# Spreading the third batch's norm and w_in's maxima over the partitions by way of DRAM instead of TensorE

## The chip, the cores and the metric

The kernel runs on one core of a Trainium2 chip. The metric is the time of one execution on the device in microseconds, median of several runs. PE stands for TensorE, DVE for VectorE, ACT for ScalarE, POOL for GpSimd and SP for the engine whose queue issues most of the DMAs.

## The reference, cut to what matters

```
# q, k, v: 8 batches x 8 heads x 576 x 64;  p: 8 x 8 x 32 x 64
def sm_attn(qq, kk, vv):                     # softmax(qq kk^T / 8) vv
    ...
p_packed = sm_attn(p, k, v)                  # 32 packed rows a head
x = sm_attn(q, p_packed, p_packed)           # 576 rows a head
h = x @ w_in                                 # 4608 x 512 @ 512 x 2048
g = h * erf(softplus(h))
out = g @ w_out                              # 4608 x 2048 @ 2048 x 512
```

All of it is float32 (the weights arrive as 64 bit floats and are cut down on the chip).

## The kernel before, in words

The second attention is a product of small softmax weights (`a2`, 128 x 576 twice) with the packed rows, so the kernel multiplies the packed rows into `w_in` first (`w_prime`, line 599: tiles `wp`) and then forms h as `a2` times `wp` (`h_half`, line 650). Each float32 operand is split into a high and a low part (`wph` and `wpl`, `a2h` and `a2l`, `gh` and `gl`, `woh`), and three products are summed. Batches 0 and 1 use a float32 format for the parts; from batch 2 on (`NB0 = 2`, "the third batch") the parts are float16, which needs scales: powers of two that come from the largest absolute norm of the packed rows and the largest entry of `w_in`.

The feed-forward part is a list of units. A unit is one batch, one half of its 576 rows and 256 of the 2048 hidden columns. `step(n, m)` (line 750) issues two groups of six matmuls for h of unit n, copies them from PSUM by ACT, issues the 24 output matmuls (`o_part`, line 711) of unit m = n - 5, and the split of g for unit m + 2. ACT's softplus and erf, and DVE's product (line 692), stand between. Units 20 to 23 are the second row half of batch 0 with hidden blocks 4 to 7 (so `gh_1_6` in the lists below belongs to unit 22), units 24 to 27 the first row half of batch 1 with the same blocks.

What else has to happen (the attention of later batches, the scales, loads of weights) is put into slots of units by a table, `slot(n, where)`. From unit 20 on nothing but the order of these calls, and a scheduler that works by a simulated time, sets the order in each engine's queue; the order in a queue is kept on the chip. Tiles come from pools: h and some scores share the two banks of `ps_h`, `wp` and the second half of the scores use `ps_m`, `gh` and `gl` have two buffers each.

The scale needs a maximum over the 128 partitions, known in every partition. `spread` (line 188) does this without PE: DVE transposes the column in blocks of 32, SP writes the four rows of 32 to DRAM (line 193, `line`), and SP reads them back into a row that is the same in all partitions (line 195, `row`). Then `two_over` (line 175) takes the row's maximum and makes a power of two of it, three DVE instructions (lines 177, 178, 180). Batches 3 to 7 and `w_out`'s maxima (`col_out`, `line_out`, `row_out`) go this way. The third batch's norm and `w_in`'s maxima (`top_in`) are turned on PE by two transposes (lines 547 and 204) into the bank `po`, from which DVE takes the maximum.

`scales(b)` (line 212) makes `rho`, `back` and `gs` from the two inverses. `w_prime_high` (line 631) multiplies by `rho` on ACT for batch 2 (line 636, `wph`), and `w_prime_low` does the same on DVE (line 645, `wpl`).

SP's queue holds, around this work, the loads of `q` for batch 2, then eight loads of 512 KB of `w_out` back from DRAM (`wox<-scratch`, line 238), then `p`, `k` and `v` of batch 3. The transfers of this queue count on eight semaphores in turn, so a transfer is issued when the one eight places ahead of it has landed.

Of the kernel before, what the change touches and what calls it, by code (L numbers as in the profile page):

```python
# [8 lines left out]
F32 = mybir.dt.float32  # L9
# [36 lines left out]
def tile_pack_attention_moe(ctx: ExitStack, tc: tile.TileContext, qT, kT, v, pT, w_in, w_out, outT):  # L46
    nc = tc.nc
    P = 128
# [17 lines left out]
    NB0 = 2  # L66
# [8 lines left out]
    cpool = ctx.enter_context(tc.tile_pool(name="const", bufs=1))  # L75
# [9 lines left out]
    ident = cpool.tile([P, P], F32, name="ident")  # L85
# [72 lines left out]
    tops, inverse, halved, pairs = {}, {}, {}, {}  # L158
# [16 lines left out]
    def two_over(dst, src):  # L175

        nc.vector.tensor_reduce(dst, src, axis=AX.X, op=ALU.max)
        nc.vector.tensor_scalar(dst, dst, TINY, None, op0=ALU.max)
        bits = dst.bitcast(U32)
        nc.vector.tensor_scalar(bits, bits, EXPONENT, EXPONENT, op0=ALU.bitwise_and, op1=ALU.bitwise_xor)  # L180

    def gather(kind):

        top = cpool.tile([P, 1], F32, name=f"top_{kind}")
        nc.vector.tensor_reduce(top[:], tops[kind][:], axis=AX.X, op=ALU.max)
        halved[kind] = top if kind == "in" else spread(kind, top[:])

    def spread(name, column):

        wide = apool.tile([P, NK], F32, name=f"col_{name}", tag="col", bufs=1)  # L190
        nc.vector.transpose(wide[:], column.to_broadcast([P, NK]))
        line = dpool.tile([P // NK, NK], F32, name=f"line_{name}", tag="line", bufs=2)
        nc.sync.dma_start(line[:], wide[:].rearrange("(q k) n -> q k n", k=NK)[:, 0, :])
        row = apool.tile([P, P], F32, name=f"row_{name}", tag="row", bufs=1)
        nc.sync.dma_start(row[:], line[:].rearrange("q n -> (q n)").unsqueeze(0).to_broadcast([P, P]))
        return row[:]

    def turn(kind, row=None):

        if row is None:  # L200
            inverse[kind] = cpool.tile([P, 1], F32, name=f"inv_{kind}")
            two_over(inverse[kind][:], halved[kind])
            return
        nc.tensor.transpose(row, halved[kind][:].to_broadcast([P, P]), ident[:])
        inverse[kind] = cpool.tile([P, 1], F32, name=f"inv_{kind}")
        two_over(inverse[kind][:], row)

    def other_way(dst, src):

# [64 lines left out]
    def is_narrow(b, j):  # L274

        return b >= NB0 + 2 or (b == NB0 + 1 and j >= 2)

    functions = []

# [66 lines left out]
    def attention(b):  # L346

        joined, third, roomy = b > NB0, b == NB0, b == 0
# [10 lines left out]
        def bank(name, single=False):  # L359

            if single:
                return [ps_h.tile([P, 512], F32, name=f"{name}_{b}_{x}", tag="ps_h")[:] for x in range(2)], None
            if name in at_o:
                d = at_o[name]
                return [ps_o.tile([P, 512], F32, name=f"{name}_{b}_{x}", tag=f"ps_o{d + x}")[:] for x in range(2)], None
            ps = ps_m.tile([P, 2, 512], F32, name=f"{name}_{b}", tag="ps_m")
            return [ps[:, 0, :], ps[:, 1, :]], ps
# [98 lines left out]
        if roomy:  # L466
# [7 lines left out]
            po, pr = bank("p")[0]  # L474
# [11 lines left out]
        else:  # L486
# [9 lines left out]
            if joined:  # L496
# [10 lines left out]
                po, pr = bank("p")[0]  # L507
# [28 lines left out]
        if b >= NB0:  # L536
# [3 lines left out]
            norm = apool.tile([P, 1], F32, name=f"norm{b}", tag="norm")  # L540
            nc.vector.tensor_reduce(norm[:], norms[:], axis=AX.X, op=ALU.max)
            if joined:
                norm_row = spread(b, norm[:])
        yield
        nc.tensor.transpose(pr[:, 2 * P:3 * P], pn, ident[:])
        if third:
            nc.tensor.transpose(po[:, P:2 * P], norm[:].to_broadcast([P, P]), ident[:])
        if b == NB0:
            turn("in", po[:, 2 * P:3 * P])
        yield  # L550
        ptt = apool.tile([P, P], F32, name=f"pt{b}", tag="pt")
        nc.scalar.copy(ptt[:], pr[:, 2 * P:3 * P])
        pt[b] = ptt
        def pack_pairs():
            inverse[b] = apool.tile([P, 1], F32, name=f"inv{b}", tag="inv")
            two_over(inverse[b][:], po[:, P:2 * P] if third else norm_row)
            if third:
                return
            sp = apool.tile([P, 1], F32, name=f"sp{b}", tag="sp")
            nc.vector.tensor_scalar(sp[:], inverse[b][:], 2.0 ** 13, None, op0=ALU.mult)  # L560
            pt16[b] = apool.tile([P, 2, P], F16, name=f"pt16_{b}", tag="pt16")
            nc.vector.tensor_scalar(pt16[b][:, 0], ptt[:], sp[:], None, op0=ALU.mult)
            nc.vector.scalar_tensor_tensor(pt16[b][:, 1], ptt[:], sp[:], pt16[b][:, 0], op0=ALU.mult, op1=ALU.subtract)

        if third:
            pack_pairs()
        yield
        ta = apool.tile([P, 2, S], F32, name=f"ta{b}", tag="big", bufs=3)
        for c2 in range(2):
            banks = bank(f"s2_{c2}", b > NB0 + 1 or (b >= NB0 and c2 == 0) or (b == 1 and c2 == 1))  # L570
            for c in range(NC):
                for r in range(2):
                    nc.tensor.matmul(banks[0][r][NK * c:NK * c + NK, 0:HT], ptt[64 * r:64 * r + 64, NK * c:NK * c + NK],  # L573
                                     q[c][64 * r:64 * r + 64, c2 * HT:(c2 + 1) * HT], start=True, stop=True)
            yield
            if roomy:
                scores.append(banks[0])
            else:
                for r in range(2):
                    nc.vector.transpose(ta[:, r, c2 * HT:(c2 + 1) * HT], banks[0][r][:, 0:HT])  # L580
                if joined and c2 == 1:
                    pack_pairs()
                yield
        tb = apool.tile([P, 2, S], F32, name=f"tb{b}", tag="big", bufs=3)
        kind = F32R if b < NB0 else F16
# [13 lines left out]
    def w_prime(b, j):  # L599

        f0, n = PIECES[j]
        if (b, j) in BESIDE:
            ps = [ps_h.tile([P, 512], F32, name=f"wp{b}_{j}_{r}", tag="ps_h") for r in range(2)]
        else:
            ps = ps_m.tile([P, 2, 512], F32, name=f"wp{b}_{j}", tag="ps_m")
            ps = [ps[:, r, :] for r in range(2)] + [ps]
        terms = ((0, 0), (0, 1), (1, 0)) if is_narrow(b, j) else (None,)
        for m, term in enumerate(terms):
            for c in range(NC):
                for r in range(2):  # L610
                    rows = slice(64 * r, 64 * r + 64)
                    if term:
                        fo = f0 % (2 * FB)
                        p, w = pt16[b][rows, term[0]], narrow[c, f0 // (2 * FB)][rows, term[1], fo:fo + n]
                    else:
                        p, w = pt[b][rows], w_in_sb[rows, c, f0:f0 + n]
                    nc.tensor.matmul(ps[r][NK * c:NK * c + NK, 0:n], p[:, NK * c:NK * c + NK], w,  # L617
                                     start=(m == 0), stop=(m == len(terms) - 1), skip_group_check=len(terms) > 1)
        raw[b, j] = ps
# [11 lines left out]
    def w_prime_high(b, j, copy=nc.scalar.copy):  # L631
        for hi, lo, ps in w_prime_parts(b, j):
            if b < NB0:
                copy(hi, ps)
            elif b == NB0 or (b, j) in BESIDE:
                nc.scalar.mul(hi, ps, 2.0 ** -15 if is_narrow(b, j) else rho[b][:])
            else:
                nc.vector.tensor_scalar(hi, ps, 2.0 ** -15 if is_narrow(b, j) else rho[b][:], None, op0=ALU.mult)
# [153 lines left out]
    def attend(b):  # L792
        if b not in gens:
            gens[b] = attention(b)
        next(gens[b])

    def slot(n, where):
        return plan.setdefault((n, where), [])
# [14 lines left out]
    f = 2  # L813
# [4 lines left out]
    for n, kind in ((22, "in"), (27, "out")):  # L818
        slot(n, 1).append((gather, kind))
    slot(28, 5).append((turn, "out"))  # L820
    slot(24, 2).append((scales, NB0))
    slot(28, 5).append((out_weights,))
    slot(32, 3).append((out_scale, NB0))
    for i, high, low in ((0, 28, 29), (1, 28, 30), (2, 29, 30), (3, 30, 31), (4, 31, 32), (5, 32, 33), (6, 32, 35), (7, 34, 37)):
# [106 lines left out]
```

## Time and profile before

| | us |
|---|---|
| median of 3 runs | 676.59 (676.27 to 678.91) |
| profiled execution | 677.14 |
| its span, first to last instruction | 675.4 |
| PE busy | 663.9 (98%) |
| DVE busy | 516.7 (77%) |
| ACT busy | 504.6 (75%) |
| POOL busy | 69.8 (10%) |

The busy share of DVE and ACT is a mean over the whole span. Between 160 and 170 us, where the third batch's scale is used, DVE is busy for 9.86 of 10 us and ACT for 9.58. The page's chain that ended last lies on PE for 84% of the span and on DVE for 7%.

### The profile page before, as it was taken

The numbers are of one execution on the slowest core, as the hardware profiler recorded it, in microseconds if no ns is written. First come the engines' busy times: TensorE is split into PE (matmuls) and PEld (weight loads), VectorE is DVE, ScalarE is ACT, GpSimd is POOL, SyncE is SP. The second block draws the span as 40 slices with busy tenths as digits, with TensorE's granted clock in tenths as the row PEclk, the third lists the DMA queues.
The fourth block names the chain that finished last, engine by engine and source line by source line (L and its number), as shares of the span: only waits on it lengthen the run. The fifth ranks groups of instructions, "written<-read, shape, count | busy, mean of one in ns | idle before, by whom it ended". The sixth has DMA issues, their size and how long they took to land.

```text
span 675.4 us, 15725 instructions
## 1 busy us (share of the span) xinstructions
PE 663.9 (98%) x6530; PEld 531.9 (79%) x6530; DVE 516.7 (77%) x836; ACT 504.6 (75%) x814; POOL 69.8 (10%) x103
## 2 busy tenths in 40 slices
PE   8999999999999999999999999999999999999998
PEld 5687999998988777777777777777777777777776
DVE  4999999988997689879976769567885768563443
ACT  2799988877779679667786878766796777777681
POOL 2032033102433100100010000100001000000000
PEclk9999999999999999999999999999999999999999
DMA  9996457249244703520052303322033100001011
GB/s 314 401 352 221 149 170 267 84 155 309 32 125 64 185 1 106 162 71 29 7 172 94 95 1 98 98 81 86 2 135 98 36 1 12 27 1 36 1 36 36
DMA packets 40503, 73.44 MB, mean 109 GB/s; under 512 B 4976, under 2 KB 17840, under 8 KB 40432
## 3 DMA queue, kind: packets, MB, share of 16 engines
q1 hardware_dynamic: 34832, 61.29, 27.7%
q0 software_dynamic: 5312, 10.56, 6.1%
q8 instruction: 51, 0.84, 0.5%
q10 hardware_dynamic: 288, 0.59, 0.2%
q14 instruction: 20, 0.16, 0.1%
HBM read 53.48 MB, written 18.94 MB: 107 GB/s over the span
## 4 chain that ended last, share of the span: by engine, by line
PE 84%; DVE 7%; ACT 3%; issue 3%; DMA 3%; POOL 1%; SPq 0%; POOLq 0%; ACTq 0%; DVEq 0%
PE o L722 52%; PE h L667 25%; PE wp L617 3%; DMA wi<-w_in 2%; PE p L450 1%; DVE hs L692 1%; PE s L573 1%; DMA k<-kT 1%; DVE gl L705 1%; PE s L420 1%; DVE w_in_sb L117 1%; DVE a2l L343 1%; DVE tops_in L165 1%; ACT L685 0%; DVE wpl L643 0%
## 5 line engine op out<-in xcount | busy, mean ns | idle before, releaser
L722 PE MATMUL o<-gh,woh 128*128 128x288 f16 x1536 | 301.0, 287 | 0.0
L722 PEld LDWEIGHTS <-woh 128*128 128x128 f16 x2304 | 223.8, 98 | 64.5 <-issue 8.8
L722 PE MATMUL o<-gl,woh 128*128 128x288 f16 x768 | 219.9, 286 | 0.0
L667 PE MATMUL h<-a2h,wph 128*128 128x288 f16 (+1 forms) x512 | 149.1, 291 | 1.0 <-DVE hs L677 0.6
L667 PE MATMUL h<-a2h,wpl 128*128 128x288 f16 (+1 forms) x512 | 147.9, 289 | 1.2 <-DVE wpl L643 1.2
L667 PE MATMUL h<-a2l,wph 128*128 128x288 f16 (+1 forms) x512 | 147.7, 289 | 0.0
L698 DVE CAST gh<-hs 128x576 f16<-128x576 f32 (+1 forms) x117 | 53.2, 455 | 98.8 <-PE o L722 98.5
L679 ACT ACTIVATE hs<-h 128x288 f32<-128x288 f32 x168 | 64.5, 406 | 85.1 <-PE h L667 85.1
L722 PE MATMUL o<-gh,wohl 128*128 128x288 f32 x448 | 98.7, 300 | 0.4 <-ACT ob L732 0.2
L705 DVE TENSOR_TENSOR gl<-hs,gh 128x576 f16<-128x576 f32 (+1 forms) x124 | 95.5, 770 | 4.5 <-ACT gh L698 0.5
L692 DVE TENSOR_TENSOR hs<-t,hs 128x576 f32<-128x576 f32 x128 | 91.6, 761 | 1.3 <-ACT t L688 1.2
L667 PEld LDWEIGHTS <-wph 128*128 128x128 f16 x768 | 74.3, 98 | 20.2 <-issue 1.0
L722 PEld LDWEIGHTS o<-gh,wohl 128*128 128x128 f32 x448 | 74.4, 188 | 7.2 <-issue 2.7
L688 ACT ACTIVATE t<-t 128x576 f32<-128x576 f32 x128 | 79.5, 674 | 0.6
L685 ACT ACTIVATE t<-hs,gs 128x576 f32<-128x576 f32 x96 | 74.5, 776 | 3.8 <-DVE hs L677 1.6
L685 ACT ACT_TABLE_LOAD x50 | 64.2, 1283 | 5.4 <-DVE hs L677 3.6
L722 PE MATMUL o<-gl,wohl 128*128 128x288 f32 x224 | 66.3, 296 | 0.1
L688 ACT ACT_TABLE_LOAD x49 | 62.9, 1283 | 0.9
L667 PEld LDWEIGHTS <-wpl 128*128 128x128 f16 x384 | 37.6, 98 | 9.5
L722 PEld LDWEIGHTS o<-gl,wohl 128*128 128x128 f32 x224 | 42.3, 189 | 0.3 <-DVE gl L705 0.3
L734 ACT ACTIVATE ob<-o,omega 128x288 f32<-128x288 f32 x48 | 21.8, 493 | 15.3 <-PE o L722 15.3
L501 POOL DMA_DIRECT2D a1m<-wide x20 | 11.8, 593 | 201.1 <-DMA wide<-a 150.5
(135 smaller groups left out, 750.2 us busy)
## 6 DMA issues: line engine op xcount, KB each, us to landing
q<-qT SPq DMA_DIRECT2D x32, 288.0 KB, 3.8
k<-kT SPq DMA_DIRECT2D x30, 288.0 KB, 5.3
wos<-w_out SPq DMA_DIRECT2D x16, 512.0 KB, 4.7
v<-v SPq DMA_DIRECT2D x29, 256.0 KB, 3.9
outT<-ob SPq DMA_DIRECT2D x48, 144.0 KB, 1.8
wi<-w_in SPq DMA_DIRECT2D x12, 512.0 KB, 7.1
outT<-ob POOLq DMA_DIRECT2D x32, 144.0 KB, 3.8
scratch<-wo POOLq DMA_DIRECT2D x16, 256.0 KB, 2.9
```

The lines of the kernel that those rows point to most:

```text
L117: nc.vector.scalar_tensor_tensor(bits, middle, 13, bits, op0=ALU.logical_shift_right, op1=ALU.bitwise_or)
L501: queue.dma_start(moved[NK * x:NK * x + NK, r], wide[r][:, t0:t0 + NCH * NK].rearrange("(c k) t -> k c t", k=NK))
L617: nc.tensor.matmul(ps[r][NK * c:NK * c + NK, 0:n], p[:, NK * c:NK * c + NK], w, start=(m == 0), stop=(m == len(terms) - 1), skip_group_che ...
L667: nc.tensor.matmul(ps[:, 0:HT], w[:, r, fo:fo + P], a[:, r, c * HT:(c + 1) * HT], start=(m == 0), stop=(m == 5))
L679: nc.scalar.mul(dst, src, 2.0 ** -18)
L685: in_turn(nc.scalar.activation(ts[n][:], rows[n][:], AF.Softplus, scale=scale))
L688: in_turn(nc.scalar.activation(ts[n][:], ts[n][:], AF.Erf))
L692: nc.vector.tensor_tensor(hs[:], ts.pop(n)[:], hs[:], op=ALU.mult)
L698: copy(ghi[:], gs[n][0][:])
L705: nc.vector.tensor_tensor(glo[:], hs[:], ghi[:], op=ALU.subtract)
L722: nc.tensor.matmul(acc[b, c, d][:, 0:HT], w[f][:, d * P:(d + 1) * P], gg[:, k, :], start=(first and k == 0 and m == 0), stop=(last and k = ...
L734: nc.scalar.mul(ob[:], acc[b, c, d][:, 0:HT], omega[b][:])
```

## The change

The norm of the third batch and the maxima of `w_in` now also go through `spread`. PE's two transposes disappear, `turn` loses its branch for PE, and `gather` calls `spread` for both kinds. `w_in`'s column is turned right after its maxima are gathered (unit 22). In the attention of the third batch, in the yield that held `pack_pairs()`, DVE now makes `w_in`'s inverse and then turns the norm's column. The norm's inverse and `scales` move from slot (24, 2) to slot (25, 1), ahead of the `wph` of slot (25, 2).

```
-        halved[kind] = top if kind == "in" else spread(kind, top[:])
+        halved[kind] = spread(kind, top[:])
...
-    def turn(kind, row=None):
-
-        if row is None:
-            inverse[kind] = cpool.tile([P, 1], F32, name=f"inv_{kind}")
-            two_over(inverse[kind][:], halved[kind])
-            return
-        nc.tensor.transpose(row, halved[kind][:].to_broadcast([P, P]), ident[:])
+    def turn(kind):
+
         inverse[kind] = cpool.tile([P, 1], F32, name=f"inv_{kind}")
-        two_over(inverse[kind][:], row)
+        two_over(inverse[kind][:], halved[kind])
...
+    packs = {}
+
+    def pack(b):
+
+        packs.pop(b)()
...
         nc.tensor.transpose(pr[:, 2 * P:3 * P], pn, ident[:])
-        if third:
-            nc.tensor.transpose(po[:, P:2 * P], norm[:].to_broadcast([P, P]), ident[:])
-        if b == NB0:
-            turn("in", po[:, 2 * P:3 * P])
...
-            two_over(inverse[b][:], po[:, P:2 * P] if third else norm_row)
+            two_over(inverse[b][:], norm_row)
...
         if third:
-            pack_pairs()
+            turn("in")
+            norm_row = spread(b, norm[:])
+            packs[b] = pack_pairs
...
-    slot(24, 2).append((scales, NB0))
+    slot(25, 1).append((pack, NB0))
+    slot(25, 1).append((scales, NB0))
```

Three places show what this moves. The first is SP's queue behind the last load of batch 2's `q`. Before, the loads of `w_out` follow at once:

```order
L407 DMA q_2_1646<-qT 128x576
L238 DMA wox_1880<-scratch 128x2x512
L238 DMA wox_1882<-scratch 128x2x512
L238 DMA wox_1985<-scratch 128x2x512
L238 DMA wox_1987<-scratch 128x2x512
L238 DMA wox_2078<-scratch 128x2x512
```

After the change the write of `w_in`'s column (`line_in`) stands ahead of them and the read of its row (`row_in`) behind the fourth:

```order
L408 DMA q_2_1646<-qT 128x576
L193 DMA line_in<-col_in 4x32
L233 DMA wox_1886<-scratch 128x2x512
L233 DMA wox_1888<-scratch 128x2x512
L233 DMA wox_1991<-scratch 128x2x512
L233 DMA wox_1993<-scratch 128x2x512
L195 DMA row_in<-line_in 128x128
L233 DMA wox_2084<-scratch 128x2x512
```

Two small transfers have come into the row of eight large ones.

The second place is the same queue behind the eighth `wox`. Before, it holds batch 3's first loads (and a `p` of batch 4), and then the pair for `w_out`'s maxima:

```order
L379 DMA p_2205<-pT 128x128
L382 DMA k_3_2207<-kT 128x576
L382 DMA k_3_2208<-kT 128x576
L379 DMA p_3005<-pT 128x128
L382 DMA k_3_2209<-kT 128x576
L382 DMA k_3_2210<-kT 128x576
L402 DMA v_3_2585<-v 64x512
L402 DMA v_3_2588<-v 128x512
L193 DMA line_out<-col_out 4x32
L195 DMA row_out<-line_out 128x128
```

After, the pair for the third batch's norm (`line` and `row`) stands among them, with two `k` and two `v` between its halves:

```order
L380 DMA p_2215<-pT 128x128
L383 DMA k_3_2217<-kT 128x576
L383 DMA k_3_2218<-kT 128x576
L380 DMA p_3015<-pT 128x128
L193 DMA line_2028<-col_2026 4x32
L383 DMA k_3_2219<-kT 128x576
L383 DMA k_3_2220<-kT 128x576
L403 DMA v_3_2595<-v 64x512
L403 DMA v_3_2598<-v 128x512
L195 DMA row_2030<-line_2028 128x128
L193 DMA line_out<-col_out 4x32
L195 DMA row_out<-line_out 128x128
```

The read of the row is the last but two of these twelve.

The third place is DVE's queue where the scale is worked out. Before, `rho` needs only what is already in SBUF, and the maxima of `w_out` (`tops_out`) come behind it:

```order
L319 TENSOR_REDUCE mx_2118<-ta_2052 128x36
L321 TENSOR_TENSOR ta_2052<-ta_2052,mx_2118 128x1152
L215 TENSOR_SCALAR rho_2121<-inv_2022,inv_in 128x1
L210 TENSOR_SCALAR back_2123<-rho_2121 128x1
L219 TENSOR_SCALAR gs_2125<-back_2123 128x1
L165 TENSOR_REDUCE tops_out<-wohl_1310 128x1
L165 TENSOR_REDUCE tops_out<-wohl_1331 128x1
L165 TENSOR_REDUCE tops_out<-wohl_1336 128x1
L698 CAST gh_1_6_2190<-hs_1_6_1843 128x576
```

After, the three maxima come first, then the norm's inverse from the row that comes from DRAM, then `rho`:

```order
L322 TENSOR_TENSOR ta_2058<-ta_2058,mx_2124 128x1152
L165 TENSOR_REDUCE tops_out<-wohl_1310 128x1
L165 TENSOR_REDUCE tops_out<-wohl_1331 128x1
L165 TENSOR_REDUCE tops_out<-wohl_1336 128x1
L177 TENSOR_REDUCE inv_2163<-row_2030 128x1
L178 TENSOR_SCALAR inv_2163<-inv_2163 128x1
L180 TENSOR_SCALAR inv_2163<-inv_2163 128x1
L210 TENSOR_SCALAR rho_2167<-inv_2163,inv_in 128x1
L205 TENSOR_SCALAR back_2169<-rho_2167 128x1
L214 TENSOR_SCALAR gs_2171<-back_2169 128x1
L697 CAST gh_1_6_2200<-hs_1_6_1843 128x576
```

The inverse of `w_in` has moved likewise: it stood ahead of the split of unit 20's g, and now stands behind it, with the turn of the norm's column, right ahead of the four transposes of the second scores (`ta<-s`, line 580). ACT's queue has the same instructions in the same order.

## Rows read from the trace of the kernel before

**Rows 1.** Page, busy us and share of the span, by engine

```profile
PE 663.9 (98%) x6530; PEld 531.9 (79%) x6530; DVE 516.7 (77%) x836; ACT 504.6 (75%) x814; POOL 69.8 (10%) x103
```

**Rows 2.** Chain that ended last, in order of time: start us, us, what

```profile
149.69 0.32 PE p L547
150.01 0.11 PE p L204
150.12 0.80 PE o L722 x6
```

**Rows 3.** Timeline of PE: start us, us, engine line op out<-in xcount

```profile
149.18 0.33 PE L545 MATMUL p<-ident,a 128*128 128x128 f32 x1
...
156.85 0.29 PE L667 MATMUL h<-a2h,wph 128*128 128x288 f32 x1
...
167.59 0.30 PE L667 MATMUL h<-a2h,wph 128*128 128x288 f32 x1
```

**Rows 4.** Timeline of SP's queue, DMA issues

```profile
145.24 5.10 SPq L238 DMA_DIRECT2D wox<-scratch  x8
...
155.13 0.33 SPq L379 DMA_DIRECT2D p<-pT  x1
...
161.43 0.34 SPq L402 DMA_DIRECT2D v<-v  x1
...
221.99 0.52 SPq L193 DMA_DIRECT2D line<-col  x1
227.89 0.33 SPq L195 DMA_DIRECT2D row<-line  x1
```

**Rows 5.** What SP's queue waited for, 150 to 162 us: total, times, longest

```profile
SPq L382 <- DMA wox<-scratch: 3.9, 4, 1.0
...
SPq L379 <- DMA wox<-scratch: 1.7, 2, 0.9
```

**Rows 6.** Issues at 152.47 and 155.13: KB, us from issue to landing

```profile
k<-kT SPq DMA_DIRECT2D x1, 288.0 KB, 11.3
...
p<-pT SPq DMA_DIRECT2D x1, 64.0 KB, 10.5
```

**Rows 7.** Landing of the six reads of a row, line 195

```profile
DMA to landing us min/median/max: 2.8/2.9/4.3
```

**Rows 8.** Busy time by stretch: PE, PEld, DVE, ACT, POOL, clock, DMA share, GB/s

```profile
167.00:169.00 2.00, 2.00 (x17) 2.00 (x16) 1.97 (x4) 1.99 (x3) 0.00 (x0) 1.00 0.20 61
```

**Rows 9.** Timeline of DVE

```profile
154.06 1.58 DVE L580 STREAM_TRANSPOSE ta<-s 128x288 f32<-128x288 f32 x4 [1.27 <-PE s L573]
...
161.38 1.86 DVE L165 TENSOR_REDUCE tops_out<-wohl 128x1 f32<-128x512 f32 x3
...
178.72 0.28 DVE L177 TENSOR_REDUCE inv_out<-row_out 128x1 f32<-128x128 f32 x1 [0.73 <-DMA row_out<-line_out]
...
179.42 0.15 DVE L231 TENSOR_SCALAR sigma<-inv_out 128x1 f32<-128x1 f32 x1
```

**Rows 10.** Timeline of ACT

```profile
162.81 1.09 ACT L636 ACTIVATE wph<-wp,rho 128x1024 f16<-128x1024 f32 x1
...
166.28 0.68 ACT L675 COPY hs<-h 128x288 f32<-128x288 f32 x2
```

**Rows 11.** Timeline of PE, its start and its last matmul

```profile
1.35 4.52 PE L860 MATMUL idle<-ident 128*128 128x128 f32 x22 [1.35 <-POOL ident masks.py:199]
...
17.24 2.95 PE L860 MATMUL idle<-ident 128*128 128x128 f32 x24
...
671.76 0.29 PE L722 MATMUL o<-gh,woh 128*128 128x288 f16 x1
```

**Rows 12.** Busy time by stretch at the end, columns as in rows 8

```profile
672.00:674.00 2.00, 0.04 (x1) 0.00 (x0) 0.00 (x0) 0.50 (x1) 0.00 (x0) 1.00 0.61 218
674.00:675.40 1.40, 0.00 (x0) 0.00 (x0) 0.00 (x0) 0.00 (x0) 0.00 (x0) 0.56 0.00 0
```

## The prediction, before the changed kernel ran

> **What bounds the kernel now.** I read the page's busy shares first. PE is busy for 663.9 of 675.4 us [rows 1], so a microsecond that PE loses in the middle of the program is lost at the end, and nearly nothing is there to make it good. Then I read the chain in order of time around the edit, to see whether PE's two removed transposes lie on it: they do [rows 2]. Then the timelines of PE, DVE, ACT and of SP's queue between 145 and 180 us, because the change takes little from PE and puts two round trips through DRAM in its place. The reader is to see three things there. PE starts the six plus six h matmuls of unit 25 at 156.85 and those of unit 27 at 167.59 [rows 3]. ACT makes the first `wph` with the scale at 162.81, and only behind it, in order, the copies of unit 26's h out of PSUM, at 166.28 [rows 10]. And SP's queue is in its fullest stretch: eight loads of 512 KB are issued within 5.1 us from 145.24 [rows 4], and each later issue waits for one of them to land [rows 5].
>
> **What it removes.** PE's transpose of pn ends at 149.18 + 0.33 = 149.51; behind it come the norm's transpose (which waited for DVE) and the one of the maxima, and the output matmuls go on at 150.12 [rows 2, 3]. Without both they go on at 149.51, so PE gains 0.61 us. ACT's copy of pt comes earlier too, which is worth nothing, since PE uses it 3 us later.
>
> **What it adds: the first round trip.** Two SP transfers, `line_in` (0.5 KB) and `row_in` (64 KB). Issuing takes about 0.5 and 0.33 us [rows 4], beside other work. What counts is the landing. A pair in the other loaded stretch shows it: the write of the column was issued at 221.99, and the read of the row, which only waits for that landing, at 227.89, so 512 bytes took over 5 us behind the loads ahead of them [rows 4]. The read itself took 2.8 us at best and 4.3 at worst [rows 7]. So small transfers here land in the order of the queue, after what is ahead of them. `row_in` stands behind the fourth `wox`, which landed at 155.1: the `p` issued at 155.13 had waited for it [rows 4, 5]. For 64 KB I add 0.4 us, as k's landing (152.47 + 11.3 = 163.8) and p's (155.13 + 10.5 = 165.6) have 352 KB in 1.8 us between them [rows 6]. With the pipe's end the row is there at 155.6; bounds are 150.6 (issued at 147.8 behind four issues, 2.8 us) and 156.5.
>
> DVE needs it behind gl of unit 20, at about 151.6, and stands until 155.6. Behind the wait on DVE are three small instructions (178.72 to 179.42 in the same sequence before, 0.70 us) and the column's turn (0.25 us), then the four transposes of the scores, which started at 154.06 and were idle 1.27 us before [rows 9]; they now start at 156.6. They free the two banks that unit 25's h uses: the first at 157.0. PE would be there at 156.85 - 0.61 = 156.24 [rows 3], so it waits 0.8 us, and the gain is gone by unit 25 (0.15 us behind the old kernel). At the early bound PE does not wait and keeps 0.61.
>
> **The second round trip.** It is `line`, `row`, the inverse and then `rho`. `line` needs the column's turn and the landing of the transfer eight places ahead, the fifth `wox`, so it goes out at about 157, behind the first two `k` and the `p`, which landed as late as 165.6 [rows 6]; it uses few rings, so I give it 164 to 166. `row` stands behind two more `k` and two `v` in the queue, and eight places behind the first `k`, which landed at 163.8; with the added 64 KB, 164.1. So SP issues `row` at 164.1 to 166, and it lands 2.8 to 4.3 us later [rows 7]: 166.9 to 170.3. I take 169.0, an issue at 164.7 plus 4.3, because the two `k` and two `v` are then still in the rings: before, the engines were busy for 0.20 of the stretch from 167 to 169, that is until about 167.4, with the last `v` issued at 161.43 [rows 4, 8], and the two reads add 128 KB.
>
> DVE gets to the inverse at about 165.5 (the three maxima ended at 161.38 + 1.86 = 163.2 [rows 9], 0.5 us of scale work is no longer ahead of them, and all is 2.5 us late from the transposes). It stands until 169.0. The inverse takes 0.70 and rho 0.21 with its gaps 0.26, so `wph` starts on ACT at 169.96 instead of 162.81. Queued behind it on ACT are the table load and the exp of the scores, and then the copies of unit 26's h, 166.28 - 162.81 = 3.47 us after wph's start [rows 10], the first done 0.37 later. PE's h of unit 27 needs those two banks. So it starts at 169.96 + 3.84 = 173.8, against 167.59: **6.2 us late**, the 0.61 and the 0.8 included. The bounds of the row give 171.7 (4.1 late) and 175.1 (7.5). DVE's split of unit 22 and `wpl` are late too, but done at about 171.6 and 174.9, ahead of PE's use of them. From there PE is the bound again; DVE is some 1.4 us behind it and has the slack of a unit, price nothing to 1.4.
>
> **The clock.** PE would be ready at 167.59 + 0.15 and stand for about 6 us. TensorE's last matmul ends at 672.05; the stretch from 672 to 674 still has a granted clock of 1.00, the level of 2.4 GHz, and that from 674 to 675.4 a mean of 0.56, so the lower level (1.2 GHz) came at about 674.2, 2.1 us after the last matmul [rows 11, 12]. At the start the first 22 dummy matmuls took 4.52 us and later 24 of them 2.95 [rows 11]: 123 ns at the upper level, hence 246 at the lower, and 4.52 us are 14.7 at the lower level, 3.6 us. So a stand of 6 us costs another half of 3.6, 1.8 us. The Trainium skill (TensorE: Matmul & The Clock Gate, What's actually happening) says that the lower level is the default and that activity lifts it. By the middle of this trace alone, where no stand is that long, the term would be nothing and the sum 6.2; by that rule it is due, and the two ends of the trace agree with it.
>
> **Sum.** 6.2 + 1.8 = 8.0 us on the profiled execution's 677.14 (span 675.4 and 1.7 around it): 685.1. The median of the runs is 0.55 lower, so 684.6.
>
> **The rivals.** *The small transfers are not held up by the large ones.* Then `row_in` lands at 150.6, PE keeps its 0.61 through unit 25, but `row` still cannot be issued before the first `k` landed, 164.1, and lands at 166.9. PE's unit 27 starts at 171.7, 4.1 late, with the clock's 1.8 only in part: 680.7 to 682.5. For it: the median of the six rows is 2.9 [rows 7]; against it: 221.99 to 227.89 [rows 4]. [...]
>
> *The scale is in time, and only the transposes' removal is left.* This is the case that isn't slower. Its place is ACT's copy of unit 26; it decides by the landing of `row`: at 162.2 or before, the copies end before 167.0 and PE waits for nothing. It then gains 0.61 us, 676.0. Against it: eight issues in turn on landings that the trace shows [rows 5]; for it: only if the large loads ahead run earlier than before.
>
> *The stand is longer or the clock costs double.* `line` lands behind the following k as well, `row` at 170.3, and the lower level lasts through two stretches of 3.6 us: 7.5 + 3.6, 687.7.
>
> **Numbers.** The forecast has 0.68, the first rival 0.15, the second 0.10, the third 0.07. What a measurement of this kernel can tell from no change is 0.5%, 3.4 us. The forecast, the first and the third lie above 680.0, all but a corner of the first; the second lies within. Faster by over 3.4 us has no mechanism, 0.02 for what I have not seen. Slower 0.88, within 0.10. The range goes from the first rival's early end, 680.4, to 687.8, the third's.
>
> **What would show it.** DVE idle before `inv<-row` (line 177) for over 2 us with the row's DMA named; `wph` of line 635 at 168 us or later; PE idle for 4 to 6 us before unit 27's h, released by ACT's copies, and a clock under 1.00 in the stretch behind it; about 4 us of DVE idle before `inv_in<-row_in`. The prediction is wrong if `wph` starts before 165, or if PE has no idle time over 1 us between 150 and 180.

## The result, and the profile after

The changed kernel takes a median of 685.87 us (684.52 to 686.91, four runs) against 676.43 for the kernel before (675.83 to 678.91, four runs): a ratio of 1.0136, 95% interval 1.0123 to 1.0150. It is slower by 1.4%, and the forecast of 684.6 (680.4 to 687.8) holds. The profiled execution took 685.98, with a span of 684.2, 8.8 longer than before.

Read the changed kernel first as the kernel before was read, by the page's busy line. PE is busy 3.8 us more [rows 1] with two instructions fewer:

```profile
PE 667.7 (98%) x6528; PEld 534.9 (78%) x6528; DVE 517.5 (76%) x838; ACT 504.8 (74%) x814; POOL 68.6 (10%) x103
```

The work is the same less two transposes, so the longer busy time is time in which PE worked slowly; what else the 8.8 holds is time in which it stood. The timeline of SP's queue, which answers to [rows 4], shows the four small transfers between the large ones (start, issue time, count):

```profile
145.21 0.62 SPq L193 DMA_DIRECT2D line_in<-col_in  x1
145.92 2.06 SPq L233 DMA_DIRECT2D wox<-scratch  x4
148.35 1.98 SPq L195 DMA_DIRECT2D row_in<-line_in  x1
150.42 2.20 SPq L233 DMA_DIRECT2D wox<-scratch  x4
153.51 0.35 SPq L380 DMA_DIRECT2D p<-pT  x1
...
158.69 0.51 SPq L193 DMA_DIRECT2D line<-col  x1
...
165.08 1.38 SPq L403 DMA_DIRECT2D v<-v  x2
166.56 0.38 SPq L195 DMA_DIRECT2D row<-line  x1
```

In DVE's timeline the two rows are what its two longest waits of this stretch end on:

```profile
157.37 0.28 DVE L177 TENSOR_REDUCE inv_in<-row_in 128x1 f32<-128x128 f32 x1 [5.75 <-DMA row_in<-line_in]
...
158.07 1.53 DVE L579 STREAM_TRANSPOSE ta<-s 128x288 f32<-128x288 f32 x4
...
170.54 0.29 DVE L177 TENSOR_REDUCE inv<-row 128x1 f32<-128x128 f32 x1 [4.17 <-DMA row<-line]
...
171.24 0.21 DVE L210 TENSOR_SCALAR rho<-inv,inv_in 128x1 f32<-128x1 f32 x1
```

ACT, waiting for `rho`, makes `wph` at 171.54 instead of 162.81, and the copies of unit 26's h come 3.50 us behind it, as they did before (3.47) [rows 10]:

```profile
171.54 1.11 ACT L635 ACTIVATE wph<-wp,rho 128x1024 f16<-128x1024 f32 x1 [5.67 <-DVE rho L210]
...
175.04 0.68 ACT L674 COPY hs<-h 128x288 f32<-128x288 f32 x2
```

PE's timeline, reduced to the first h matmul of units 25, 26, 27 and 28, has both stands in its brackets. Before, units 25 and 27 began at 156.85 and 167.59 [rows 3], and neither row shows a wait:

```profile
158.57 0.40 PE L666 MATMUL h<-a2h,wph 128*128 128x288 f32 x1 [2.15 <-DVE ta L579]
...
166.17 0.29 PE L666 MATMUL h<-a2h,wph 128*128 128x288 f32 x1
...
175.47 0.40 PE L666 MATMUL h<-a2h,wph 128*128 128x288 f32 x1 [4.38 <-ACT hs L674]
...
183.58 0.29 PE L666 MATMUL h<-a2h,wph 128*128 128x288 f32 x1
```

The table by stretch (columns as in [rows 8]; the clock is the third number from the right) shows the lower level behind each stand. Over 159 to 162 and over 176 to 179 it is 0.50, which is 1.2 GHz, and PE is busy for the whole of both:

```profile
159.00:162.00 3.00, 3.00 (x14) 3.00 (x14) 2.97 (x7) 0.79 (x2) 0.85 (x1) 0.50 1.14 285
...
164.00:175.00 11.00, 7.09 (x54) 6.86 (x52) 6.62 (x16) 5.29 (x7) 0.00 (x0) 1.00 0.38 109
...
176.00:179.00 3.00, 3.00 (x15) 3.00 (x14) 2.96 (x5) 2.39 (x4) 0.00 (x0) 0.50 0.00 0
```

The kernel before has unit 28's h at 174.06:

```profile
174.06 0.29 PE L667 MATMUL h<-a2h,wph 128*128 128x288 f32 x1
```

So unit 25 is 1.7 late, unit 27 is 7.9 late and unit 28 is 9.5 late. Of these 9.5, 0.9 come back much later: PE's list of waits before has one of 0.9 us ahead of `p` (line 450, near 435) for which no engine is named, and after there is none in that place. No run here shows what ends it.

### The profile page after: what moved, and what is told of

It reads as the page before. It is cut to its first block, busy times and chain, and to the rows that moved or that the text cites. A ratio compares the mean times of both kernels' runs of the same rounds, so it can differ in the third digit from the quotient of the medians.

```text
span 684.2 us, 15724 instructions
## 1 busy us (share of the span) xinstructions
PE 667.7 (98%) x6528; PEld 534.9 (78%) x6528; DVE 517.5 (76%) x838; ACT 504.8 (74%) x814; POOL 68.6 (10%) x103
## 4 chain that ended last, share of the span: by engine, by line
PE 82%; DVE 6%; DMA 5%; ACT 3%; issue 2%; POOL 1%; SPq 0%; POOLq 0%; ACTq 0%; DVEq 0%
PE o L721 51%; PE h L666 25%; PE wp L616 3%; DMA wi<-w_in 2%; DMA row_in<-line_in 1%; PE p L451 1%; DVE hs L691 1%; PE s L572 1%; DMA k<-kT 1%; PE s L421 1%; DMA row<-line 1%; DVE gl L704 1%; DVE w_in_sb L117 1%; DVE a2l L344 0%; DVE tops_in L165 0%
## 5 line engine op out<-in xcount | busy, mean ns | idle before, releaser
L666 PEld LDWEIGHTS h<-a2h,wph 128*128 128x128 f32 x128 | 24.8, 194 | 10.0 <-ACT hs L674 4.6
```

What stands on the lines that cost most here:

```text
L666: nc.tensor.matmul(ps[:, 0:HT], w[:, r, fo:fo + P], a[:, r, c * HT:(c + 1) * HT], start=(m == 0), stop=(m == 5))
```

## Experiments

The theory was that of the prediction: each row is late because its transfer shares the stretch with large loads, DVE and then ACT stand for it, and PE's lower clock comes on top. Four rivals were put against it: that the two trips share the loss, that DVE's new order is the cause, that four more transfers delay the large loads, and that SP's queue, rather than the DMA engines, is the bottleneck. A table of all runs; "27 to 28" is the time between the first h matmuls of units 27 and 28, and the row is in use when DVE's inverse starts. Each ratio is to the kernel before as it ran beside that kernel, with medians of 676.43, 675.94, 676.42 and 676.28. The other columns come from one profiled execution each, in which unit 23's first h lies between 144.33 and 146.84, so a difference of some tenths between two kernels says little.

| run | median us | ratio to before (95%) | `inv_in` at | `inv` at | PE's stands before units 25 / 27 | 27 to 28 |
|---|---|---|---|---|---|---|
| before | 676.43 | | | | 0 / 0 | 6.47 |
| changed | 685.87 | 1.0136 (1.0123 to 1.0150) | 157.37 | 170.54 | 2.15 / 4.38 | 8.11 |
| maxima only | 678.27 | 1.0031 (1.0019 to 1.0043) | 155.94 | | 0.77 / 0.95 | 6.57 |
| norm only | 685.04 | 1.0129 (1.0111 to 1.0148) | | 169.57 | 0 / 6.75 | 8.71 |
| on POOL's queue | 688.34 | 1.0175 (1.0154 to 1.0195) | 156.02 | 171.59 | 1.10 / 8.32 | 8.99 |
| wox later | 683.85 | 1.0118 (1.0101 to 1.0136) | 153.47 | 165.04 | 0 / 3.23 | 8.07 |
| PE filled, long | 689.33 | 1.0180 (1.0161 to 1.0199) | 156.00 | 169.13 | 0 / 0 | 6.54 |
| PE filled, short | 685.35 | 1.0130 (1.0114 to 1.0145) | 155.04 | 169.45 | 0 / 2.32 | 8.10 |
| transfers unused | 676.55 | 1.0000 (0.9988 to 1.0012) | | | 0 / 0 | 6.47 |
| small first | 678.21 | 1.0026 (1.0013 to 1.0039) | 153.31 | 163.84 | 0 / 0 | 6.57 |
| before, wox later | 676.86 | 1.0003 (0.9992 to 1.0014) | | | 0 / 0 | 6.47 |
| small first, wox together | 677.22 | 1.0016 (1.0007 to 1.0024) | 152.22 | 162.75 | 0 / 0 | 6.57 |

Each edit below is cut to its lines, and is one of the changed kernel where nothing else is said.

**Each half alone.** With the maxima only:

```diff
+        if third:
+            nc.tensor.transpose(po[:, P:2 * P], norm[:].to_broadcast([P, P]), ident[:])
...
-            two_over(inverse[b][:], norm_row)
+            two_over(inverse[b][:], po[:, P:2 * P] if third else norm_row)
...
+            pack_pairs()
             turn("in")
-            norm_row = spread(b, norm[:])
-            packs[b] = pack_pairs
...
-    slot(25, 1).append((pack, NB0))
```

> Only w_in's maxima go by way of DRAM; the third batch's norm stays on PE, so line and row are gone from SP's queue and the scale is worked out in unit 25 as in the changed kernel. Theory (each landing is waited for by itself): the first stand stays as in the changed kernel, inv_in at about 157.4, unit 25's h at 158 to 159 after a stand of about 2 us with one fall of the clock behind it; no stand of more than 1 us before unit 27's h, which comes 1.7 late from the stand plus 1.7 from the clock less what the later slack gives back: 3 to 4 us over the kernel before, about 679.5. Rival (the first trip's lateness is swallowed by DVE's and ACT's slack by unit 28): 676 to 677.5. Rival (the moved scale and maxima on DVE cost, not the trips): over 683.

With the norm only:

```diff
-        halved[kind] = spread(kind, top[:])
+        halved[kind] = top if kind == "in" else spread(kind, top[:])
...
-    def turn(kind):
+    def turn(kind, row=None):
...
+        if row is not None:
+            nc.tensor.transpose(row, halved[kind][:].to_broadcast([P, P]), ident[:])
...
-        two_over(inverse[kind][:], halved[kind])
+        two_over(inverse[kind][:], halved[kind] if row is None else row)
...
+        if third:
+            turn("in", po[:, 2 * P:3 * P])
...
-            turn("in")
```

> Only the third batch's norm goes by way of DRAM; w_in's maxima stay on PE. Theory: no stand before unit 25's h (156.6 to 157.2); the row lands at 167 to 170, rho and wph behind it, unit 27's h at 172 to 175.5 after a stand of 4 to 7 us and one fall of the clock behind it: 6.5 to 9.5 us over the kernel before, 683 to 686, nearly the whole loss, since the second landing hides the lateness of the first. Rival (the two trips add up, each with its own share): 681 to 682.5, the rest of the 9.4 being the first trip's 3 to 4.

DVE's wait and PE's two stands with the maxima only:

```profile
155.94 0.29 DVE L177 TENSOR_REDUCE inv_in<-row_in 128x1 f32<-128x128 f32 x1 [3.89 <-DMA row_in<-line_in]
```

```profile
157.05 0.40 PE L667 MATMUL h<-a2h,wph 128*128 128x288 f32 x1 [0.77 <-DVE ta L580]
169.00 0.40 PE L667 MATMUL h<-a2h,wph 128*128 128x288 f32 x1 [0.95 <-ACT hs L675]
```

The same two with the norm only, and the clock behind the stand:

```profile
169.57 0.29 DVE L177 TENSOR_REDUCE inv<-row 128x1 f32<-128x128 f32 x1 [6.82 <-DMA row<-line]
```

```profile
174.51 0.61 PE L669 MATMUL h<-a2h,wph 128*128 128x288 f32 x1 [6.75 <-ACT hs L677]
```

```profile
170.00:174.00 4.00, 0.00 (x0) 0.00 (x0) 3.83 (x11) 3.39 (x3) 0.00 (x0) 0.83 0.00 0
174.00:179.00 5.00, 4.49 (x18) 4.34 (x18) 4.86 (x9) 3.41 (x7) 0.00 (x0) 0.50 0.00 0
```

The norm's trip alone costs 9.1 us (685.04 - 675.94, the kernel before on that chip), and the maxima's alone 2.3. They don't add up to the 9.4 of both, because the first lateness is spent inside the second wait. That the two trips share the loss is out. For the maxima the expectation of 679.5 was 1.2 too high: `row_in` was in use at 155.9 and not at 157.4, PE stood for 0.77 us before unit 25 and 0.95 before unit 27, and the clock did not fall. The norm's came out as expected. That DVE's new order is the cause is out as well: `scales` still stands in unit 25 in the first of these kernels, and it loses 2.3 us, not 9; and in the last kernel of the table, which has that order too, PE stands before neither unit. How much of the 2.3 is the order's isn't shown.

**Another queue.** The four small transfers go out on POOL's queue:

```diff
+        queue = nc.gpsimd if name in ("in", NB0) else nc.sync
...
-        nc.sync.dma_start(line[:], ...)
+        queue.dma_start(line[:], ...)
...
-        nc.sync.dma_start(row[:], ...)
+        queue.dma_start(row[:], ...)
```

> The changed kernel, with the four small transfers (line_in, row_in, line, row) issued from POOL's queue in place of SP's. Theory (they are late because they stand behind 512, 288 and 256 KB loads on SP's queue): each lands 2.8 to 5 us after it is issued, row_in by about 154, row by about 163, no stand over 1 us before unit 25's or unit 27's h, and the time is 675.5 to 678. Rival (the DMA engines themselves are shared, at a share of about 1.1 in this stretch, so that another queue does not help): row at 167 or later, 682 to 686. Rival (DVE's order and not the landing): 684 to 687 with the landings early.

POOL's timeline has the two issues of the second trip, and the view of DMA issues the time from issue to landing of `row_in`, `row` and `line` (KB, us):

```profile
161.01 0.87 POOL L194 DMA_DIRECT2D line<-col  x1
168.33 0.61 POOL L196 DMA_DIRECT2D row<-line  x1 [6.46 <-issue]
```

```profile
row_in<-line_in POOLq DMA_DIRECT2D x1, 64.0 KB, 6.1
row<-line POOLq DMA_DIRECT2D x1, 64.0 KB, 3.2
...
line<-col POOLq DMA_DIRECT2D x1, 0.5 KB, 6.7
```

My theory as I put it here, that their place in SP's queue is what makes them late, is wrong: 688.34 is 12.4 over the kernel before. 64 KB took 6.1 us, and 512 bytes 6.7, on a queue on which no large load stands. The queue alone isn't the reason: a second read of 64 KB on it took 3.2 us at 168.33, when the busy share of the DMA engines was 0.24 (168 to 172 us). From 150 to 156, where `row_in` took 6.1, that share was 1.03, and it was 0.98 from 150 to 170. For `line` the case is less clean, because a store of 144 KB of outputs stands 0.5 us ahead of it on POOL's queue. The rival was right in its mechanism and 2.3 us low: `line` also went out late, at 161.01, behind that store. The Trainium skill (DMA: Bandwidth & Descriptors, Issuing engines are not separate DMA queues) says that transfers from any issuing engine end up on the same 16 DMA engines; this run, with 6.1 us on POOL's queue beside the loads of SP's, agrees.

**Fewer loads ahead.** The loads of `wox` come three units later, in the changed kernel and in the kernel before; two `wox`, a `p` and a `k` then stand ahead of `row_in` instead of four `wox`, and two `wox` come only at 179:

```diff
-        slot(22 + i // 2, 1).append((whole, i))
+        slot(25 + i // 2, 1).append((whole, i))
```

> The changed kernel, with the eight 512 KB loads of wox issued three units later (two each from unit 25 on), so that fewer large loads stand ahead of row_in. Theory: row_in lands about 3 us earlier (152 to 155), the first stand is under 1 us and the clock stays up there; the row still has four wox, two k and two v near it and lands at 166 to 171, so the second stand stays at 3 to 7 us with one fall of the clock: 681 to 686. If wox is then late for its own readers, more. Rival (the first trip's lateness is due to its own round trip and not to the loads ahead): row_in at 157 as before and 685 to 687.

> The kernel before, with the eight loads of wox three units later and nothing else: the measure for the run with wox later. Theory: wox has slack, 675.5 to 677. Rival (wox late costs by itself, and the run with wox later owed part of its 7.9 us over the kernel before to that): 678 or more.

DVE's two waits in the changed kernel with `wox` later:

```profile
153.47 0.29 DVE L177 TENSOR_REDUCE inv_in<-row_in 128x1 f32<-128x128 f32 x1 [2.25 <-DMA row_in<-line_in]
...
165.04 0.29 DVE L177 TENSOR_REDUCE inv<-row 128x1 f32<-128x128 f32 x1 [2.58 <-DMA row<-line]
```

`row_in` came 3.9 us earlier, and the first stand was gone; the row came 5.5 earlier, more than I had said, and the second stand was 3.23. The profiled execution is the fastest of its five (680.42; the others took 683.19 to 685.40, with a lower mean clock, 0.993 to 0.995 against 0.997), so the table's stands show the mildest case; the median, 683.85, lies where it was expected. In the kernel before, late `wox` costs nothing that can be told from no change. So large loads near the small transfers make these late.

**The transfers without the wait.** The kernel before, with both columns turned and all four transfers made, and their rows left unread (the edit is one of the kernel before):

```diff
         halved[kind] = top
+        if kind == "in":
+            spread(kind, top[:])
...
+            spread(b, norm[:])
```

> The kernel before, with the changed kernel's two turned columns and four small transfers added in the same places of SP's queue, and their rows read by nobody: PE's two transposes still give the norm and the maxima. Theory (only the wait for the rows costs): 675.5 to 677.5, with the rows landing at 155 to 157.5 and 167 to 170.5 as in the changed kernel, and k, p and v about 1 us later than before. Rival (four more transfers in the full stretch delay the loads that batch 3 and the split of w_out need): 679 or more.

PE's list of waits from 145 to 250 us has nothing of a row in it:

```profile
PE o L725 <- ACT ob L735: 0.2, 1, 0.2
PE p L549 <- DVE norm L543: 0.2, 1, 0.2
```

The transfers cost nothing that can be told: 676.55 against 676.42. Their rows were about as late as in the changed kernel: `row_in` landed 7.8 us after its issue at 148.86, at 156.7, and `row` was issued at 166.38 against 166.56 (its landing isn't in the profile). So the change costs what is waited for, and nothing measurable by its traffic.

**The clock.** Extra matmuls ahead of the h matmuls of units 25 and 27, 16 and 46 of the identity, were meant to fill PE's stands:

```diff
+    FILL = {25: 16, 27: 46}
...
+        if n in FILL:
+            bank = acc[(0, 0, 0) if n == 25 else (0, 1, 0)]
+            for _ in range(FILL[n]):
+                nc.tensor.matmul(bank[:, 384:512], ident[:], ident[:], start=True, stop=True, ...)
```

> The changed kernel, with extra matmuls of the identity into columns of two banks that nothing reads (16 in unit 25 and 46 in unit 27, ahead of the h matmuls), so that PE is busy where it stood. Theory (part of the loss is PE's clock, which falls after a stand): the granted clock is 1.00 from 150 to 190, unit 27's h starts where the landing of the row lets it, at 174 to 176.5, and unit 28's h 6 us behind that instead of 8.1; the time is 1.5 to 2.5 below the changed kernel's 685.9, 683.4 to 684.4. Rival (the clock's fall costs nothing beyond the stand itself): 685.5 to 687.

In this kernel the extra matmuls change the result, other than the expectation says, so it is read for its times alone. PE's timeline and the clock:

```profile
155.94 3.73 PE L755 MATMUL o<-ident 128*128 128x128 f32 x32
170.24 10.44 PE L755 MATMUL o<-ident 128*128 128x128 f32 x92
```

```profile
174.00:179.00 5.00, 5.00 (x47) 5.00 (x47) 4.86 (x8) 2.28 (x4) 0.00 (x0) 1.00 0.01 3
```

They took twice what I had reckoned and held PE until 180.7, long after the row (169.13), so the total, 689.33, says nothing on the clock. The run still has the answer: at a clock of 1.00 throughout, units 27 and 28 lie 6.54 us apart. A second kernel filled with 10 and 36 matmuls of zeros, added to an open sum:

```diff
+    FILL = {25: 10, 27: 36}
...
+                nc.tensor.matmul(bank[:, 0:HT], nought[:, 0:P], nought[:], start=False, stop=False, ...)
```

> As the run that kept PE busy, whose extra matmuls took 3.7 and 10.4 us and so outlasted the stands that they were to fill: here 10 in unit 25 and 36 in unit 27, of zeros added to an open accumulator (nothing of the result changes), about 1.3 and 4.7 us. Theory (part of the loss is PE's clock): the granted clock is 1.00 from 150 to 190, unit 27's h starts at 173.5 to 176 where the row lets it, unit 28's h 6.5 us behind it and not 8.1, and the time is 682.5 to 684.5. Rival (the fall costs nothing beyond the stand): 685.5 to 687.

```profile
155.51 1.40 PE L757 MATMUL o<-nought 128*128 128x288 f16 x10
167.48 4.58 PE L757 MATMUL o<-nought 128*128 128x288 f16 x36
174.39 0.40 PE L668 MATMUL h<-a2h,wph 128*128 128x288 f32 x1 [2.32 <-ACT hs L676]
```

```profile
174.00:179.00 5.00, 4.61 (x34) 4.17 (x42) 4.86 (x8) 3.29 (x7) 0.00 (x0) 0.66 0.00 0
```

Here the filling was too short: 2.32 us of the second stand were left, the clock fell all the same, and 27 to 28 took 8.10. The first stand was filled and the first fall gone, and the time is that of the changed kernel within half a microsecond (685.35). By itself the total is nearer the rival, but it doesn't decide: the first fall is swallowed by the second wait, and the second was not prevented. What the fall costs is read from the table's last column. The seven kernels whose clock stayed up behind unit 27 take 6.47 to 6.57 there, the three with one fall 8.07 to 8.11: 1.5 to 1.6 us, at the same work.

**The small transfers first.** The last two kernels ask whether the route can be had without the wait. The norm's column is turned at once, and `wox`, and `p` and `k` of batch 3, may only go out behind the last small transfer:

```diff
-            if joined:
+            if joined or third:
                 norm_row = spread(b, norm[:])
...
+    def after_small(load):
+        then(load.ins, small[NB0])       # wox, p and k of batch 3: behind the row
...
-        slot(22 + i // 2, 1).append((whole, i))
+        slot(25 + i // 2, 1).append((whole, i))
```

> The changed kernel, with the norm's column turned as soon as the norm is there, and all four small transfers ahead of every large load of the stretch on SP's queue: line_in, row_in, line, row, then wox, p, k and v (wox three units later, as in the run with wox later). Theory (the transfers are late only because of the large loads issued ahead of them): row_in lands by 152 and row by 157, no stand over 1 us before unit 25's or unit 27's h, the clock stays at 1.00, and the time is 675 to 677, the 0.6 us of PE's two transposes being too little to be told. Rival (two trips take too long even with nothing ahead): row at 162.5 or later and 678 or more. Second rival (the large loads, now 7 us later, are what PE waits for): a stand at k, v or the halves of w_out after 170, 678 or more.

DVE no longer waits for either row, but for the third one, that of `w_out`:

```profile
153.31 0.28 DVE L177 TENSOR_REDUCE inv_in<-row_in 128x1 f32<-128x128 f32 x1
...
163.84 0.27 DVE L177 TENSOR_REDUCE inv<-row 128x1 f32<-128x128 f32 x1
...
183.75 0.28 DVE L177 TENSOR_REDUCE inv_out<-row_out 128x1 f32<-128x128 f32 x1 [3.98 <-DMA row_out<-line_out]
```

The 9.4 us shrink to 1.8 (678.21 against 676.42): both stands and the fall are gone, which is the theory's claim. Its time, 675 to 677, was missed by a wait that I had not thought of. Two `wox` go out right behind `row_out`, and stores of outputs beside it, and it takes 4.8 us. DVE's products behind that wait are late, ACT stands 3.1 us for them, PE 1.1 for ACT's copies of h, and unit 31 comes 1.9 later than before. The profiled execution took 680.71, 2.5 over the median of its twelve, so these waits may be longer than in most. With all `wox` in one stretch behind the row (an edit of the kernel just shown):

```diff
-        slot(25 + i // 2, 1).append((whole, i))
+        slot(25 + i // 4, 1).append((whole, i))
```

> As the run with the small transfers first, but with all eight wox behind the row in one stretch, so that none is issued with row_out (there two wox went out 0.4 us behind row_out, which then took 4.8 us; DVE stood 4.0 for it, and unit 31's h came 1.9 late). Theory (in that stretch too the wait for a small transfer beside large ones is the whole cost): row_out lands 2.8 us after its issue, no stand over 1 us on PE between 150 and 200, and the time is 675 to 676.5. Rival (the large loads, 7 us later, are the cost): 677.5 or more, with a stand at wox, k or v.

```profile
152.53 0.33 SPq L200 DMA_DIRECT2D row<-line  x1
...
177.75 0.33 SPq L200 DMA_DIRECT2D row_out<-line_out  x1
```

```profile
181.26 0.29 DVE L177 TENSOR_REDUCE inv_out<-row_out 128x1 f32<-128x128 f32 x1 [2.58 <-DMA row_out<-line_out]
```

PE's list of waits of the same kernel has one of 1.3 us where the kernel before has one of 0.2:

```profile
PE o L728 <- ACT ob L738: 1.3, 1, 1.3
```

677.22 against 676.28: 1.0016 (1.0007 to 1.0024). From unit 23 to unit 30, PE kept what the two transposes gave: 38.02 us between their first h matmuls, 38.54 in the kernel before. Then `row_out` still took 3.5 us, beside outputs that are stored then, and unit 31 came 0.5 later; and the wait for ACT's copy of an output, which the kernel with the small transfers first and the kernel before with late `wox` have as well, made another unit 1.1 longer (6.26 between h matmuls, 5.17 before). The expectation, 675 to 676.5, was missed by 0.7; these two waits are what the trace shows for it, but no run takes them away. The 1.1 needn't show in a total: the kernel before with late `wox` has it too, and its 0.4 over the kernel before can't be told from no change. No version beats the kernel before: the gain to be had is 0.6 us, and in both kernels that got it, with the large loads sent later, other waits took more than that.

## Why the prediction was right, step by step

- **PE's gain of 0.61.** Right: unit 24's h started at 150.17 instead of 150.76, 0.59 earlier, and nothing of it was left by unit 25.
- **The first trip.** Right in its place, too small in the changed kernel's own execution: 0.8 us of stand forecast, 2.15 measured, as `row_in` came at 157.4 against 155.6, beyond my bound of 156.5. This landing varies: with the same loads ahead of it, `row_in` was there 10.6, 11.1, 11.3, 11.4 and 12.2 us behind the issue of `line_in` in five kernels. The changed kernel's own is the last of these. In its trace the landing of `row_in` is 16 events: 15 came by 155.42, near the forecast, and the last at 157.34; in the other four kernels the last came 0.01 to 0.44 us behind the 15th. What held that one part up isn't shown. With 11.4 (the maxima only) the stand was 0.77, as forecast. I had not allowed for a fall of the clock after this stand. Neither changed the sum, since the second wait swallows what the first one loses.
- **The second trip.** Right in its chain from SP's issue on: DVE's wait, `rho`, `wph`, the copies of unit 26's h, PE. From DVE's start on the row to PE's h it took 4.93 us (forecast 4.80). The size was off by 1.7: unit 27 was 7.9 late and not 6.2. SP could issue `row` at 166.56 only, against 164.7. The forecast tied this issue to the landing of the first `k`; it named the two `v` that stand ahead of `row`, but not what they wait for. By the rule of eight places the first `v` waits for the eighth `wox`, and this one, issued at 152.18, took 12.8 us to land (15 of its 16 events by 163.09, the last at 165.02), so the `v` went out from 165.08; before, the second `v` was out at 161.43 [rows 4]. The row was in use at 170.54, just outside the bound of 170.3.
- **The clock.** Right in kind and nearly in size: once for the second stand, 1.5 to 1.6 us (forecast 1.8). The stand itself was 4.38 us and not 6, because PE came to it at 171.09 and not at 167.74, after the first stand and its fall.
- **Sum.** 7.9 late at unit 27, 9.5 at unit 28, 8.8 at the end, against a forecast of 8.0. That the total came nearer than unit 28 is luck: the 0.9 that comes back later was in no term. The reason I gave, that small transfers "land in the order of the queue", was too narrow, as on another queue they are as late; and the pair it was read from doesn't show it. The `k` issued at 221.52, next ahead of that `line`, took 7.6 us, so it landed at 229.1, behind the `line`, which had landed by 227.89 [rows 4]. What the pair does show is a small transfer that is slow beside large ones.
- **The rivals.** *Not held up* is shown wrong: 6.1 and 6.7 us on a queue of their own, 2.8 with nothing ahead. *The scale in time* needed the row by 162.2; it came so early only where the large loads were sent behind it. *Longer, clock double* came near in the changed kernel (row at 170.54, two falls), and the kernel with the small transfers on POOL's queue went beyond it. The range is a little wider than the rivals' own sums, which give 680.7 and 687.7 for its ends 680.4 and 687.8; 685.87 lies inside either.

## What to carry to other kernels

Price a round trip through DRAM by what else is in the DMA engines at that time, not by its bytes: here 64 KB took 2.8 us alone and 4 to 9 beside large loads, and 512 bytes 5.9 on SP's queue [rows 4] and 6.7 on POOL's. Before an instruction is made to wait for such a trip, look for what stands behind it in order on its engine; most of the loss came from copies of a finished unit that stood behind one scaled weight on ACT, and from the clock's fall after that stand. And of two waits in a row only the later landing counts, so mending the first alone gains next to nothing: without the maxima's trip the norm's still costs 9.1 of the 9.4 us.

## What the runs showed that I had not expected

- PE's clock fell after stands of 2.15, 2.32, 3.23 and 4.38 us and did not after stands of 0.77, 0.95 and 1.10. In the changed kernel it fell only when PE was already at work again: the stretch from 164 to 175 has 1.00, that from 176 to 179 has 0.50. After stands of 6.75 and 8.32 us it fell while PE still stood (0.83 over 170 to 174 with the norm alone), and 27 to 28 took 8.71 and 8.99.
- Transfers issued behind a small one seem to delay it too. `row_out` took 4.8 us from issue to use with two `wox` issued 0.4 us behind it and stores of outputs beside it, 3.5 in the last kernel with the stores and no `wox`; `row_in` took 2.8 in the first of these kernels, with neither.
- The first trip, with the same loads ahead of its 64 KB read, varied by 1.6 us from kernel to kernel (10.6 to 12.2 us from the issue of `line_in` to the row), so one execution's stand is a weak measure of such a trip.
